# Another order of the steps from the 380th on, and state products in the upper columns of their banks

## The chip, the cores and the metric

The kernel runs on one core of a Trainium2 chip. The metric is the device time of one execution in microseconds (us), the median of several runs. The engines are named as in the profile: PE is TensorE (matmuls, with PEld for its weight loads), DVE is VectorE, ACT is ScalarE, POOL is GpSimd, and SP only issues DMAs (SPq is its queue). Each engine works through its own instructions strictly in the order in which they were written; between engines there are semaphores.

## The reference

Two blocks follow each other. The first is a gated linear attention with a state of 48 x 48 for each of 4 x 8 heads, over 768 tokens; the second is a two-layer network with a hard-swish gate, over 3072 tokens.

```python
state = alpha[:, :, t, :, None] * state + np.einsum('bhd,bhe->bhde', k[:, :, t], v[:, :, t])
y[:, :, t] = np.einsum('bhd,bhde->bhe', q[:, :, t], state)
...
h = x @ w_in                       # 3072 x 384 by 384 x 2048
g = h * np.clip(h + 3.0, 0.0, 6.0) / 6.0
return (g @ w_out).astype(np.float32)   # 2048 x 384
```

x is y with its heads side by side, 384 columns for each token. All values are float32.

## The kernel before

**Chunks and groups.** The attention goes by chunks of 128 tokens: 24 chunks j = 0 to 23, six for each of the four batches. Two chunks make a group g = j // 2 of 256 tokens for the network: 12 groups. From group 2 on (and in the second layer from group 1) the network's matrix products are done by a scheme with fewer multiplications: 20 small products in place of 24 (M, with sums of x and of weights ahead and sums of outputs behind), and 7 in place of 8 in the second layer (P).

**Steps.** The program is a text of 1788 words. Each word names a step, with its arguments behind points; `run` (L749) executes them in the order of the text under `tc.manual_schedule()`, so each engine gets its instructions in just that order, and the framework sets the semaphores that the data need. For the banks of PSUM it counts two accesses as depending on each other when they touch one bank, whatever the columns. So `M.10.9` is the tenth product of group 10, and where it stands among the PE words is when PE gets to it. The words that this text speaks of, with their lines:

- Attention, loads: `la`, `lk`, `lq` (L248; alpha, k and q of a chunk, four DMAs from chunk 6 on), `lv` (L267; v).
- Attention, on DVE: `ca`, `tk`, `tq` (L286; transposes from chunk 6 on), `r` and `p` (L309, L320; scans), `k` and `q` (L332; products with the scans), `kt` (L391; k turned back). `kw` (L393) writes the turned k to memory and `kr` (L400) reads it back by token, four DMAs each.
- Attention, products: `sc` (L338, matmuls in L346) makes the scores of a chunk in two banks, `m` (L349, L356) masks them on DVE. `u` (L422, matmuls in L429) makes the state's products of a chunk in one or two banks, `sm` (L434, L439) adds them to the state on DVE, `st` (L407, L409) decays the state on POOL, `sv` (L412, L419) places it on ACT, `qa` (L360, L366) places q on ACT. `ya` and `yb` (L448, L455) make the chunk's output y, `cy` (L461) keeps it as x on ACT.
- First layer: `xc` (L586) is one sum of x on DVE, `y` (L577) one sum of weights on DVE, `M` (L592, L600) one product, `n` (L604, L606) a copy of a product on ACT, `o` (L608; L537, L539 or L541) a sum of products on DVE, `e` (L619, L494) and `h` (L623, L498) the gate on ACT and DVE.
- Second layer: `s` (L658; L647, L664) is a sum of gated values on DVE, `P` (L685, L703) one product, `K` (L706; L682, L709) a copy on ACT, `G` (L717; L720 on ACT or L723 on DVE) an output quarter, `O` (L725) its store.
- `z` (L529, L532): dummy matmuls of the identity.

**Banks.** PSUM has eight banks of 512 float32 columns here: `banks` t0 to t3 for the attention (the last numbers of `sc`, `u`, `ya` name them) and `bank_m` m0 to m3 for the network (the last number of `M` or `P` that begins a sum). A score product takes columns 0 to 255 of its bank; y takes 0 to 383.

**What sets the order around the change.** Nothing but the text: from its 380th word (counted from zero, `y.19` in L782) it interleaves the attention of chunks 6 to 23 with the network of groups 1 to 11. The last steps are the second layer of group 11:

```python
               s.11.3.9 P.11.3.2 K.11.0.0 s.11.2.14 P.11.2 o.11.3.1 K.11.2 o.11.2.1 e.11.2.0 h.11.2
               s.11.4 e.11.3.1 h.11.3 P.11.1 G.11.0.2 s.11.5 O.11.0 K.11.1 P.11.4 G.11.1.0 P.11.5
               G.11.2.1 O.11.2 P.11.6 G.11.3.2 O.11.1 O.9.2 O.11.3""")
```

Of the kernel before, what the change touches and what calls it, by code (L numbers as in the profile page):

```python
# [17 lines left out]
def kernel(  # L18
# [33 lines left out]
    B, H, S, D = q.shape  # L52
# [4 lines left out]
    NP = H // 2  # L57
# [3 lines left out]
    G = 2  # L61
    GT = G * C
    HB = C // 2
# [42 lines left out]
    for r in range(2):  # L106
# [11 lines left out]
    st, half_st, sm = (consts.tile([C, NP, D], FP, tag=name, name=name)  # L118
                       for name in ("st", "s1", "sm"))
# [302 lines left out]
    def update(j, *at):  # L422
        for b, i in enumerate(at):
            ps_t["u", j, b] = banks[i][:, 0 : NP * D].rearrange("r (p n) -> r p n", p=NP)
        for p in range(NP):
            for a in range(2):
                for b in range(len(at)):
                    half = slice(HB * b, HB * b + HB)
                    nc.tensor.matmul(ps_t["u", j, b][64 * a : 64 * a + D, p],  # L429
                                     kb_t[j][half, p, 64 * a : 64 * a + D],  # L430
                                     v_t[j][half, b, 2 * p + a, 0:D],
                                     start=True, stop=True)
# [321 lines left out]
    with tc.manual_schedule():  # L754
# [3 lines left out]
               dx.0 w.2 d2.2 kb.1.0 ck.1 lq.1 r.2 sm.0.1 st.1 tq.1.2 q.1 d3.2 z.0.3 d1.2 dx.2  # L758
               lv.1.1 u.1.3.1 sv.1.0 sm.1.0 p.2 sm.1.1 sc.1.0.2 m.1 ya.0.3 yb.0 cy.0 lq.2 w.1 d1.1
               tq.2.1 q.2 d4.2 lk.2 tk.2.3 k.2 fa.2.0 d4.0 st.2 sc.2.0.2 d2.1 d3.1 m.2 dx.1 d4.1  # L760
               qa.1.1 lk.3 la.3 ta.3.1 ca.3 la.4 fa.0.1 sv.1.1 w.3 r.3 ta.4.3 ca.4 r.4 tk.3.1 k.3
               kb.2.0 qa.1.0 d2.3 ya.1.2 yb.1 cy.1 fa.1.2 lq.3 ck.2 d1.3 p.3 d3.3 lv.2.2 u.2.3.2
               sm.2.0 d4.3 fb.2 tq.3.1 q.3 fb.1 qa.2.0 sm.2.1 sv.2.0 st.3 fr.0.2.0 fg.0.2 lk.4
               tk.4.0 sv.2.1 w.5 d2.5 k.4 d3.5 d1.5 qa.3.0 d4.5 qa.2.1 sc.3.1.3 m.3 w.6 d2.6 d1.6
               d3.6 d4.6 lv.3.0 lq.4 w.7 kb.3.2 fb.0 f.0.3.3 kb.4.0 ya.2.1 ck.3 u.3.3.2 sm.3.0
               fr.0.3.1 fg.0.3 fr.0.1.0 fg.0.1 qa.3.1 sv.3.0 sm.3.1 p.4 d2.7 sv.3.1 d1.7 d3.7 d4.7
               f.0.5.0 fr.0.5.1 fr.0.0.0 fg.0.5 fg.0.0 tq.4.3 ck.4 la.5 ta.5.2 f.0.6.3 ca.5 w.4
               d2.4 ya.3.0 yb.3 cy.3 fr.0.6.1 yb.2 cy.2 w.9 d2.9 q.4 qa.4.1 d1.4 d1.9 dx.4 la.6 w.8
               d3.4 r.5 lk.5 w.10 d3.9 p.5 ca.6 fg.0.6 d4.9 w.12 lq.5 lv.4.1 d2.8 d3.8 f.0.7.2 d1.8
               st.4 d4.8 d4.4 w.11 fr.0.7.0 fg.0.7 f.1.7.0 fr.1.7.1 fg.1.7 sc.4.0.2 m.4 f.1.1.1  # L770
               fr.1.1.0 fg.1.1 f.1.3.3 fr.1.3.1 d2.10 d1.10 tk.5.3 f.1.0.2 d2.12 d3.10 d4.10 w.13
               fg.1.3 fr.1.0.0 fg.1.0 k.5 d3.12 lq.6 f.1.6.0 f.1.2.1 u.4.1.0 sm.4.0 d1.12 d4.12
               sv.4.0 qa.4.0 ya.4.2 fr.1.6.1 fg.1.6 w.15 tq.5.3 fa.4.3 sv.4.1 d2.11 kb.5.1 d2.13
               fr.1.2.0 f.1.4.2 fr.1.4.1 d1.11 sm.4.1 q.5 r.6 d3.11 d3.13 fg.1.4 d4.11 lv.5.0 lk.6
               tq.6 p.6 d2.15 d3.15 fg.1.2 d1.13 d4.13 sc.5.0.3 yb.4 f.1.5.0 fr.1.5.1 fg.1.5 tk.6
               m.5 b.1.0.2 fb.4 b.1.1 d1.15 d4.15 st.5 y.5 w.14 la.7 lk.7 cy.4 d2.14 qa.5.1 ck.5
               b.0.0.1 fr.0.4.0 d3.14 k.6 q.6 ca.7 fg.0.4 d1.14 d4.14 x.0 y.1 y.10 b.0.1 y.0 y.2
               u.5.2 P.1.0.0 K.1.0 qa.5.0 sv.5.0 qa.6.1 P.1.1.3 b.0.2 b.1.2 kb.6.0 ya.5.3 y.6
               s.1.0.0 sm.5.0 sv.5.1 G.1.0.0 tk.7 s.1.1.1 s.1.2.3 x.1 yb.5 cy.5 b.1.3 sc.6.1.2
               lv.6.2 ck.6 u.6.3.0 s.1.3.2 x.2 P.1.2 b.0.3 K.1.1 y.7 s.1.4 s.1.5 y.11 y.3 r.7  # L780
               xc.2.1 x.3 y.4 y.8 xc.2.3 k.7 xc.2.0 xc.2.4 y.9 y.12 y.16 y.13 y.15 P.1.3.3 K.1.2
               P.1.4 bo.1 P.1.5 xc.2.5 G.1.1.1 P.1.6 y.14 y.17 y.19 xc.2.6 sm.6.0 G.1.2.2 y.20  # L782
               M.2.0.2 lv.12.1 la.8 O.1.1 O.1.0 ca.8 y.18 y.21 y.23 so.1 G.1.3.3 n.2.0.8 bo.0 lq.7
               lv.7.0 O.1.2 m.6 xc.2.2 xc.2.10 xc.2.7 tq.7 r.8 p.7 xc.2.8 sv.6.1 M.2.15.3 M.2.1
               kb.7.3 n.2.1.9 M.2.16 M.2.2 n.2.2.10 M.2.7.0 n.2.7.11 sm.6.1 xc.2.9 q.7 p.8 M.2.3
               M.2.4 n.2.4.12 M.2.8 o.2.0.0 M.2.5 n.2.5.13 qa.7.0 sv.6.0 st.7 lk.8 O.1.3 lq.8 lk.9
               la.9 la.10 tk.8 tq.8 lq.10 lq.9 ya.6.1 yb.6 M.2.9 z.1.3 M.2.18.1 o.2.1.0 e.2.1.1
               M.2.10 cy.6 ck.7 sc.7.0.2 u.7.1.3 n.2.10.14 M.2.11 qa.7.1 ca.9 la.11 y.22 M.2.6.2
               h.2.1 q.8 m.7 e.2.0.0 h.2.0 n.2.11.15 qa.6.0 n.2.18.10 qa.8.1 M.2.12 M.2.19
               n.2.12.12 M.2.13 sm.7.0 sv.7.1 r.9 k.8 o.2.3.0 sv.7.0 ya.7.0 y.24 o.2.5.0 n.2.13.12  # L790
               o.2.2.0 yb.7 cy.7 sc.8.1.2 xc.3.1 o.2.2.1 e.2.2.1 xc.3.3 o.2.3.1 M.2.14 xc.3.4
               xc.3.0 xc.3.5 o.2.4.0 xc.3.7 xc.3.6 o.2.6.0 P.2.0.1 M.3.0.2 M.2.17 h.2.2 o.2.6.1
               e.2.3.0 h.2.3 o.2.7.0 n.3.0.12 M.3.1 n.3.1.9 e.2.5.1 M.3.7.0 n.3.7.13 xc.3.8 o.2.7.1
               K.2.0.3 xc.3.2 kt.8 e.2.6.0 h.2.6 tk.9 M.3.2 n.3.2.10 e.2.4.0 P.2.1 h.2.4 h.2.5
               s.2.0.14 e.2.7.0 G.2.0.1 h.2.7 M.3.3 M.3.4 n.3.4.8 k.9 s.2.1.11 M.3.8 o.3.0.0 ca.10
               kt.9 P.2.3.3 s.2.2.15 s.2.3.14 lv.8.2 kw.8 kr.8 lk.10 sm.7.1 xc.3.9 M.3.5 n.3.5.11
               K.2.2 e.3.0.1 xc.3.10 M.3.9 o.3.1.0 P.2.2 K.2.1 u.8.0.3 M.3.18.2 s.2.5 M.3.10
               n.3.10.14 n.3.18.15 e.3.1.0 s.2.4 P.2.4 tq.9 h.3.0 st.8 sv.8.0 M.3.11 n.3.11.8 tk.10
               p.9 sm.8.0 q.9 r.10 k.10 qa.9.0 qa.9.1 m.8 sm.8.1 h.3.1 M.3.19 o.3.5.0 kt.10 P.2.5
               G.2.2.0 st.9 M.3.12 sc.9.0.1 qa.8.0 n.3.12.10 o.3.3.0 kw.9 lv.9.0 kr.9 sv.8.1  # L800
               u.9.2.3 sm.9.0 sv.9.1 sv.9.0 G.2.1.2 sm.9.1 st.10 M.3.15.2 M.3.16 M.3.6.3 M.3.13 m.9
               o.3.4.0 o.3.6.0 tq.10 n.3.13.10 o.3.2.0 e.3.4.1 ya.8.2 yb.8 ya.9.3 yb.9 cy.9 M.3.14
               M.3.17 cy.8 xc.4.1 P.2.6 e.3.5.0 G.2.3.3 o.3.2.1 xc.4.3 h.3.4 xc.4.4 o.3.6.1 xc.4.5
               xc.4.0 xc.4.6 e.3.2.1 M.4.0.0 n.4.0.10 P.3.0.1 xc.4.7 o.3.7.0 p.10 h.3.5 o.3.3.1
               xc.4.8 M.4.7.3 M.4.1 xc.4.2 h.3.2 o.3.7.1 K.3.0.2 lk.11 O.2.2 tk.11 e.3.6.0 e.3.3.1
               h.3.3 P.3.1 e.3.7.1 n.4.1.13 M.4.2 ca.11 q.10 h.3.6 r.11 k.11 h.3.7 n.4.7.15 lv.10.2
               lv.11.0 kw.10 sc.10.0.1 kr.10 G.3.0.0 u.10.3.2 sm.10.0 qa.10.1 n.4.2.14 M.4.3 M.4.4
               M.4.8 s.3.0.9 xc.4.9 s.3.2.12 s.3.1.11 P.3.3.2 n.4.4.8 M.4.5 o.4.0.0 e.4.0.0 sv.10.1
               sm.10.1 xc.4.10 kt.11 O.2.0 O.2.3 lq.11 m.10 s.3.3.9 s.3.5 M.4.9 o.4.1.0 P.3.2
               sv.10.0 st.11 n.4.5.11 K.3.2 la.13 M.4.18.0 p.11 tq.11 lk.12 tk.12 K.3.1 M.4.10  # L810
               n.4.10.9 q.11 qa.10.0 n.4.18.12 e.4.1.1 la.12 s.3.4 ca.12 h.4.0 r.12 P.3.5 G.3.2.1
               h.4.1 M.4.11 P.3.4 n.4.11.8 M.4.12 n.4.12.14 qa.11.0 M.4.19 p.12 G.3.1.3 lq.12 kw.11
               O.2.1 tq.12 kr.11 u.11.3 sc.11.0.2 sv.11.0 O.3.1 lk.13 P.3.6 qa.11.1 M.4.6.2 G.3.3.2
               k.12 o.4.3.0 m.11 sm.11.0 sv.11.1 kt.12 M.4.13 n.4.13.14 q.12 o.4.3.1 e.4.3.0
               o.4.2.0 o.4.6.0 h.4.3 o.4.2.1 ya.10.1 ya.11.0 yb.10 yb.11 cy.11 cy.10 xc.5.1 ca.13
               xc.5.3 M.4.15.1 M.4.16 M.4.14 P.4.0.2 o.4.4.0 M.4.17 xc.5.4 o.4.5.0 xc.5.0 xc.5.5
               M.5.0.0 o.4.6.1 K.4.0.3 e.4.2.1 h.4.2 P.4.1 qa.12.1 e.4.4.0 xc.5.6 o.4.7.0 h.4.4
               o.4.7.1 tk.13 n.5.0.14 M.5.1 e.4.7.1 h.4.7 e.4.5.0 xc.5.2 h.4.5 xc.5.7 G.4.0.3
               e.4.6.1 h.4.6 s.4.1.12 s.4.0.11 xc.5.8 r.13 xc.5.9 xc.5.10 k.13 kw.12 kr.12 la.14
               sc.12.2.3 u.12.0.1 sm.12.0 n.5.1.13 M.5.2 n.5.2.15 M.5.7.1 n.5.7.8 P.4.3.3 s.4.2.9  # L820
               kt.13 lk.14 lq.13 O.3.0 O.3.3 lv.13.2 kw.13 O.4.0 lq.14 tq.13 lq.15 M.5.3 M.5.4
# [117 lines left out]
```

## Time and profile before

| What | us |
|---|---|
| runs of the kernel | 537.21, 537.83, 538.51 (median 537.83) |
| the profiled execution | 537.71 |
| its span, from the first to the last instruction | 535.6 |
| PE busy in the span | 523.6 |
| DVE busy in the span | 475.1 |
| ACT busy in the span | 259.7 |
| first PE step behind the 380th word (M.2.0) starts | 125.42 |
| end of the last matmul | 532.69 |

An instruction's row gives its start and its length in us, then engine, line, operation, the tiles written and read, and how many were merged in the row; in brackets stands how long the engine was idle ahead of it and what ended that. PE's matmuls overlap: a row of sixteen L703 matmuls is 2.76 us long, but the next row starts 2.60 us behind its start. So times of PE are taken here from start to start.

### The profile page before, as it was taken

The page shows a single profiled execution, that of the slowest core. Times are in us where ns is not written, and L with a number is a line of the kernel's source. Part 1 is how long each engine was busy: PE and PEld are TensorE (multiplying, and loading weights), DVE is VectorE, ACT ScalarE, POOL GpSimd, SP SyncE. Part 2 cuts the span into 40 slices and gives each one's busy share as a digit, 9 for nine tenths or more (in the row PEclk, how much of TensorE's full clock was granted, in tenths as well). Part 3 has the DMA queues.
Part 4 walks back from the last instruction along what each step waited for, and adds up shares of the span by engine and source line. Part 5 has one row for each costly group of instructions (what it writes and reads, how often), then busy time and mean ns, then how long its engine had stood idle before and what let it go on. Part 6 is the DMA issues. An engine that isn't in the chain of part 4 may idle for free.

```text
span 535.6 us, 15166 instructions
## 1 busy us (share of the span) xinstructions
PE 523.6 (98%) x6306; PEld 497.0 (93%) x6306; DVE 475.1 (89%) x839; ACT 259.7 (48%) x513; POOL 50.4 (9%) x71
## 2 busy tenths in 40 slices
PE   7799999999999999999999999999999999999997
PEld 7698886789999999999999999999999999999996
DVE  6999989999999899989999899999999898595381
ACT  3889864302753644543644444642634545553240
POOL 5333435000000000000010000000000000000000
PEclk9999999999999999999999999999999999999999
DMA  9998877006515155254354355055354042100001
GB/s 175 214 250 263 205 218 164 9 1 162 151 28 121 29 120 134 51 139 90 92 118 104 89 122 141 20 126 124 85 137 103 17 97 48 43 3 1 15 16 37
DMA packets 124100, 54.40 MB, mean 102 GB/s; under 512 B 83328, under 2 KB 116864, under 8 KB 124032
## 3 DMA queue, kind: packets, MB, share of 16 engines
q1 hardware_dynamic: 124032, 53.44, 42.4%
q8 instruction: 49, 0.80, 0.7%
q14 instruction: 19, 0.16, 0.1%
HBM read 44.50 MB, written 8.91 MB: 100 GB/s over the span
## 4 chain that ended last, share of the span: by engine, by line
PE 64%; DVE 20%; SPq 5%; DMA 3%; issue 3%; ACT 2%; POOL 2%; DVEq 0%; ACTq 0%; POOLq 0%
PE m_ps L703 28%; PE m_ps L600 24%; PE m_ps L478 4%; SPq L262 3%; PE t_ps L455 3%; DVE R L309 2%; DVE g_sb L498 2%; DVE A L356 2%; DMA v<-in_v_dram 1%; PE t_ps L346 1%; PE m_ps L516 1%; PE t_ps L429 1%; DVE g_sb L537 1%; DVE q L332 1%; DVE t L286 1%
## 5 line engine op out<-in xcount | busy, mean ns | idle before, releaser
L703 PE MATMUL m_ps<-w,g_sb 128*128 128x192 f32 x704 | 122.1, 327 | 0.7 <-ACT m_ps L709 0.6
L606 ACT COPY g_sb<-m_ps 128x512 f32<-128x512 f32 x110 | 63.5, 584 | 113.8 <-PE m_ps L600 97.4
L703 PEld LDWEIGHTS m_ps<-w,g_sb 128*128 128x128 f32 x704 | 113.7, 190 | 1.8 <-ACT m_ps L709 0.9
L703 PE MATMUL m_ps<-rings,g_sb 128*128 128x192 f32 x528 | 91.6, 327 | 0.6 <-ACT u L682 0.6
L703 PEld LDWEIGHTS m_ps<-rings,g_sb 128*128 128x128 f32 x528 | 85.3, 190 | 1.0 <-ACT u L682 0.9
L600 PE MATMUL m_ps<-xc,w 128*128 128x128 f32 x640 | 82.8, 277 | 0.5 <-DVE w L541 0.5
L600 PEld LDWEIGHTS m_ps<-xc,w 128*128 128x128 f32 x640 | 77.5, 192 | 1.7 <-issue 0.6
L494 ACT ACTIVATE r<-g_sb,half 128x512 f32<-128x512 f32 x80 | 56.7, 722 | 29.5 <-DVE g_sb L541 11.7
L498 DVE SCALAR_TENSOR_TENSOR g_sb<-r,g_sb 128x512 f32<-128x512 f32 x80 | 53.6, 683 | 7.2 <-ACT r L494 6.8
L600 PE MATMUL m_ps<-xT,raw 128*128 128x128 f32 x400 | 52.6, 278 | 1.0 <-ACT g_sb L606 0.9
L600 PEld LDWEIGHTS m_ps<-xT,raw 128*128 128x128 f32 x400 | 48.6, 192 | 2.0 <-ACT g_sb L606 1.4
L409 POOL TENSOR_TENSOR st<-sm,R 128x192 f32<-128x192 f32 x20 | 12.9, 644 | 354.4 <-DVE sm L439 305.6
L647 DVE TENSOR_TENSOR g_sb<-g_sb 128x512 f32<-128x512 f32 (+1 forms) x55 | 42.0, 792 | 1.4 <-PE m_ps L703 1.1
L600 PE MATMUL m_ps<-xT,w 128*128 128x128 f32 x320 | 42.0, 276 | 0.0
L600 PEld LDWEIGHTS m_ps<-xT,w 128*128 128x128 f32 x320 | 39.3, 192 | 0.1
L366 ACT COPY A<-q 48x256 f32<-48x256 f32 x88 | 35.6, 404 | 4.9 <-DVE q L332 3.7
L356 DVE TENSOR_TENSOR A<-t_ps,mask 64x256 f32<-64x256 f32 x96 | 36.0, 413 | 0.4
L478 PE MATMUL m_ps<-xT,w 128*128 128x256 f32 x144 | 32.8, 382 | 0.1
L600 PE MATMUL m_ps<-xc,raw 128*128 128x128 f32 x240 | 31.8, 276 | 0.0
L309 DVE TENSOR_TENSOR_SCAN R<-t,ones 128x516 f32<-128x516 f32 x24 | 29.6, 1235 | 1.1 <-ACT t L300 1.0
L478 PEld LDWEIGHTS m_ps<-xT,w 128*128 128x128 f32 x144 | 26.7, 190 | 3.8 <-POOL w L217 0.2
L600 PEld LDWEIGHTS m_ps<-xc,raw 128*128 128x128 f32 x240 | 29.6, 192 | 0.1
(105 smaller groups left out, 724.8 us busy)
## 6 DMA issues: line engine op xcount, KB each, us to landing
raw<-in_moe_w_out_dram SPq DMA_DIRECT2D x8, 768.0 KB, 5.2
raw<-in_moe_w_in_dram SPq DMA_DIRECT2D x6, 768.0 KB, 6.7
v<-in_v_dram SPq DMA_DIRECT2D x48, 96.0 KB, 3.0
out_dram<-oh SPq DMA_DIRECT2D x44, 96.0 KB, 1.7
far<-kq SPq DMA_DIRECT2D x64, 64.0 KB, 2.2
kb<-far SPq DMA_DIRECT2D x64, 64.0 KB, 2.0
aq<-in_alpha_dram SPq DMA_DIRECT2D x36, 96.0 KB, 2.4
qq<-in_q_dram SPq DMA_DIRECT2D x36, 96.0 KB, 2.4
```

The source lines that it names most:

```text
L262: nc.sync.dma_start(out=to[BLK * o : BLK * (o + 1), :, 0 : V * D - skip], in_=t[o // 2, :, :, skip : V * D])
L309: nc.vector.tensor_tensor_scan(out=reverse(R, n - 1, n), data0=reverse(ax, n, n), data1=reverse(ones, n, n), initial=0.0, op0=ALU.mult, op ...
L356: nc.vector.tensor_tensor(out=to[:, a], in0=sc[a][half], in1=mask[half, half].unsqueeze(1).to_broadcast([HB, NP, HB]), op=ALU.mult)
L366: nc.scalar.copy(out=to[:, a], in_=Q_t[j][64 * a : 64 * a + D, :, half])
L455: nc.tensor.matmul(y_of(j, (i + 1) // 2, p)[:, HB * b : HB * b + HB], vb[:, p, e : e + 32], A_t[j][:, b, 2 * p + a], start=(b == 0 and i = ...
L478: nc.tensor.matmul(h[:, f], w1[:, kk, o : o + C], xT_t[g][:, kk], start=(kk == 0), stop=(kk == KT - 1))
L494: nc.scalar.activation(out=to, in_=h, func=AF.Relu, bias=half, scale=1.0 / 6.0)
L498: nc.vector.scalar_tensor_tensor(out=to, in0=r, scalar=1.0, in1=h, op0=ALU.min, op1=ALU.mult)
L600: nc.tensor.matmul(acc[g][i][:, f * C : (f + 1) * C], spots[w][:, f * C : (f + 1) * C], x_of(g, x), start=(first and f == 0), stop=last, s ...
L606: nc.scalar.copy(out=slots[z], in_=acc[g][i])
L647: nc.vector.tensor_tensor(out=out, in0=in0, in1=in1, op=ALU.subtract)
L703: nc.tensor.matmul(to[g], a, rhs[:, f], start=(first and f == 0), stop=(last and f == HF - 1), skip_group_check=True)
```

## The change

Two things change. `update` writes the state's products into columns 256 to 447 of their banks; they were in columns 0 to 191.

```diff
     def update(j, *at):
         for b, i in enumerate(at):
-            ps_t["u", j, b] = banks[i][:, 0 : NP * D].rearrange("r (p n) -> r p n", p=NP)
+            ps_t["u", j, b] = banks[i][:, NP * HB : NP * (HB + D)].rearrange(
+                "r (p n) -> r p n", p=NP)
         for p in range(NP):
```

(NP is 4, HB 64, D 48.) This adds a line, so that lines behind L424 have a number higher by one afterwards.

And the words from the 380th on stand in another order. Both texts have the same 1788 steps; the first 380 are the same words (on other line breaks). Behind them no step is added or removed, and 46 steps have another bank at their end: 16 of `ya`, 16 of `sc`, 14 of `u`. The start of the new part, and places that the text speaks of:

```diff
-               P.1.4 bo.1 P.1.5 xc.2.5 G.1.1.1 P.1.6 y.14 y.17 y.19 xc.2.6 sm.6.0 G.1.2.2 y.20
-               M.2.0.2 lv.12.1 la.8 O.1.1 O.1.0 ca.8 y.18 y.21 y.23 so.1 G.1.3.3 n.2.0.8 bo.0 lq.7
-               lv.7.0 O.1.2 m.6 xc.2.2 xc.2.10 xc.2.7 tq.7 r.8 p.7 xc.2.8 sv.6.1 M.2.15.3 M.2.1
...
+               la.8 xc.2.2 xc.2.6 y.19 G.1.3.3 so.1 y.20 G.1.2.2 y.18 M.2.0.2 bo.0 y.21 M.2.15.3
+               y.23 sm.6.0 n.2.0.8 z.1.3 M.2.1 M.2.16 xc.2.8 n.2.1.9 xc.2.7 M.2.2 kb.7.3 p.7 lk.8
...
```

In words, for the rest: the dummy `z.1.3` stood between M.2.9 and M.2.18 and stands ahead of M.2.1. Score and state products of a chunk, which had banks of their own, share banks in many chunks (`u.7.1.3 sc.7.1.3`, `u.12.3.0 sc.12.3.0`, `u.14.3.0 sc.14.3.2`, `u.20.1.2 sc.20.1.0`). Chunk 21's part is `u.21.3.2 sc.21.1.0 n.9.11.11 M.9.15.3 sm.21.0 M.9.12 G.8.1.0 lk.23 ya.20.3 yb.20 m.21 sm.21.1` and, seven words on, `ya.21.1 yb.21`. The end is

```python
P.11.3.2 O.10.3 s.11.4 P.11.2 P.11.1 s.11.5 K.11.1 P.11.4 G.11.0.2 K.11.2 G.11.1.0
O.11.1 P.11.5 O.11.0 G.11.2.1 P.11.6 O.11.2 G.11.3.2 O.11.3
```

Most steps have moved by some tens of words or fewer, some loads, stores and placements on ACT by over a hundred.

## The prediction

> **What bounds the kernel now.** I read the busy shares first, then the busy times by stretch, the waits of TensorE (PE), the waits of VectorE (DVE), and the timeline where a wait stood out.
>
> ```profile
> PE 523.6 (98%) x6306; PEld 497.0 (93%) x6306; DVE 475.1 (89%) x839; ACT 259.7 (48%) x513; POOL 50.4 (9%) x71
> ...
> 240.00:280.00 40.00, 40.00 (x471) 39.60 (x472) 38.78 (x71) 17.40 (x35) 1.82 (x3) 1.00 0.42 96
> 320.00:360.00 40.00, 40.00 (x513) 39.41 (x511) 38.01 (x70) 19.30 (x42) 0.80 (x1) 1.00 0.40 96
> 400.00:440.00 40.00, 40.00 (x520) 39.11 (x519) 37.29 (x69) 17.95 (x38) 1.03 (x2) 1.00 0.32 71
> 480.00:500.00 20.00, 20.00 (x150) 20.00 (x149) 10.96 (x18) 7.12 (x14) 0.00 (x0) 1.00 0.00 1
> ```
>
> In the stretches the columns after the length are PE, PE weight loads, DVE, ACT, POOL. PE hardly rests from 120 us on, and its granted clock is 1.00 throughout. But DVE is at least 93% busy until 440 us, and only behind 460 us has it room: two engines bound this part, and PE sets the end only while DVE keeps up.
>
> ```profile
> PE m_ps L600 <- ACT g_sb L606: 0.9, 1, 0.9
> PE m_ps L703 <- ACT u L682: 0.6, 1, 0.6
> PE m_ps L703 <- ACT m_ps L709: 0.6, 2, 0.4
> PE m_ps L600 <- DVE w L541: 0.5, 1, 0.5
> ```
>
> These are all the named waits of PE matmuls from 94 us on: 2.6 us. I price them by start-to-start times: a group of eight L600 matmuls takes 0.89 us, sixteen of L703 take 2.60. What exceeds that is lost: 0.63 us at 126.3 (M.2.15 to M.2.1), 0.27 at 155.2 (M.3.2 to P.2.1), 0.32 at 195.9 (in P.3.1), 1.06 at 277.7 (P.5.1 to M.6.2), 0.41 at 443.1 (to P.9.1) and 0.79 at 521.2 (P.11.1 to P.11.4), 3.48 in all. Passing to the small matmuls (L346, L429, L455) and back costs about 0.1 us each way (a group of eight takes 0.99 ahead of them and 1.00 behind them).
>
> **The first term, a filler moved into a hole.**
>
> ```profile
> 126.31 1.06 PE L600 MATMUL m_ps<-xT,raw 128*128 128x128 f32 x8
> 127.84 1.13 PE L600 MATMUL m_ps<-xc,w 128*128 128x128 f32 x8 [0.47 <-DVE w L541]
> ...
> 137.71 0.83 PE L532 MATMUL m_ps<-ident 128*128 128x128 f32 x6
> ```
>
> M.2.1 waits until 127.84 for a weight sum on DVE. The dummy z.1.3 (six L532, 137.71 to 138.38, 0.67 us) now stands just ahead of M.2.1. PE is free at 127.20, the dummy ends at 127.87, and 0.60 us is saved where it stood. On DVE the sums ahead of it change by one short xc added and one sm put behind (0.24 for 0.31), so it is not later.
>
> **The second, the tail.**
>
> ```profile
> 521.23 2.76 PE L703 MATMUL m_ps<-w,g_sb 128*128 128x192 f32 x16
> 524.03 0.32 ACT L720 COPY oh<-m_ps 128x192 f32<-128x192 f32 x1 [3.65 <-PE m_ps L703]
> 524.24 0.33 ACT L682 COPY u<-m_ps 128x192 f32<-128x192 f32 x1
> 524.62 2.87 PE L703 MATMUL m_ps<-rings,g_sb 128*128 128x192 f32 x16 [0.63 <-ACT u L682]
> ```
>
> P.11.4 overwrites what K.11.1 copies (L682), and ACT reaches that copy only behind the output copy G.11.0 (L720), which waits for P.11.1. In the new order K.11.1 stands ahead of G.11.0: its input is ready 2.60 us earlier, at the end of P.11.2, so the copy lies beside P.11.1. DVE, counted from the last M.11.14 with 0.63 to 0.68 per step, has s.11.4 some 3 us ahead of P.11.4. Saved: 0.79.
>
> **The third, fewer passages.** PE's new order has 26 stretches of small matmuls behind step 380 for 28: 2 x 0.2 = 0.4 us.
>
> **The fourth, the other holes.** 0.27 + 0.32 + 1.06 + 0.41 = 2.06 us. Each is a short chain from PE over ACT or DVE back to PE. The new order has as many chains that the PE work between leaves less than 0.9 us to spare (22 for 22, counted with the mean durations of the readers' groups). Between 0 and 2.06 of this goes.
>
> If all went, PE alone would give 0.60 + 0.79 + 0.4 + 2.06 = 3.85 us less. The profiled execution took 537.71 us, 0.12 under the median of the runs (537.83), with a span of 535.6. So the floor is 533.9.
>
> **What works against it: DVE's queue.** The same DVE work stands in another order, and PE must not pass a step before DVE has done all that is queued ahead of its input. I added DVE's work behind step 380 in both orders with durations from back-to-back rows (two h steps 1.29 us, a scan 1.15, a transpose 1.03, four mask products 1.51), and PE's with those above. The before trace then tells at what time DVE had done so much, and when PE had.
>
> At P.8.2, 279.0 us of PE work stands ahead in both orders; ahead of its input s.8.3 stand 289.2 us of DVE work before and 291.1 after. At ya.21 it is 296.8 of PE against 306.4 of DVE before, 293.3 against 305.4 after: PE comes there at the time 427.0 of the old trace, DVE ends its mask at 430.1, 3.1 us late. The worst is M.10.9, which waits for o.10.0.0: 319.4 us of PE work (454.1) against 331.0 of DVE work (457.6), 3.5 us late, where the old order had 3.6 us to spare. Other late places are 1.8 us at P.9.1 and 1.2 at M.8.0, covered by the worst. (P.8.2 reads s.8.3 only in its second half, 1.3 us in, and is just not late.)
>
> This takes DVE to idle as before. It idled 15.7 us between 120 and 440 (320 less the busy times of the stretches). Its largest named waits, from 94 to 430 us:
>
> ```profile
> DVE g_sb L498 <- ACT r L494: 4.2, 5, 1.5
> DVE g_sb L537 <- PE m_ps L600: 2.0, 3, 1.0
> DVE oh L723 <- PE m_ps L703: 1.5, 1, 1.5
> DVE oh L723 <- ACT A L366: 1.4, 1, 1.4
> DVE xc L537 <- ACT xT L464: 1.0, 1, 1.0
> ```
>
> They are waits for inputs that PE and ACT make; a DVE that runs 1 to 3 us later meets them less. From 320 us on, where the new order has it late, the ones above 0.35 us are 1.09, 1.04, 0.43, 0.40, 1.49 and 0.54, 5.0 in all. The cut in idle lies between 0 (the waits come back at other steps) and 6.6 (PE's floor: 3.5 + 0.6 + 0.4 + 2.06). I take four fifths of 5.0: 4.0. That pays the 3.5 and leaves 0.5 of the terms ahead of 454 us; the 0.79 comes behind it. The sum: 537.71 + 3.5 - 4.0 - 0.79 = **536.4 us**.
>
> **The bank move.** update() now writes columns 256 to 447 of its bank, score products 0 to 255. It changes no instruction's size: cost of itself 0. It lets PE write both into one bank with no wait on a reader between. The built program's waits show the price: in chunks 7, 12, 14 and 20 the first sum of state (L439) waits for the score matmuls in the shared bank, up to 0.51 us (L346, 302.06 to 302.58) each, 2.0 us of DVE's idle at most, 0 where DVE has other work until then. No row of before shows a shared bank.
>
> [...]
>
> **Queues of SP and POOL.** The 16 chunks' k go through memory (kt on DVE, kw, kr on SP, then u). Before, the last read was issued 5.7 us or more behind kt and landed 2.0 later: 7.7 us at least. By the ledger the time from kt to u falls from 12.3 us at least to 8.8 (chunk 23), 9.6 (13), 9.8 (19), 9.9 (18): all hidden, with 1.1 us at the closest. Loads of alpha, k and q keep 14 us or more between the freeing of their buffer and use. The stores that moved on SP (the longest wait of SP is 39.8 us, behind the last load) stand behind outputs that are long done or in the tail. POOL (9% busy) hides st: 0.
>
> **Rivals.**
> - DVE stays as idle as before and PE waits at ya.21 and M.10.9. The early terms vanish in that wait: 537.71 + 3.5 - 0.79 = 540.4. For it: the late DVE is sure by the count. Against: waits on inputs shrink when the reader comes later. It turns slower than before once less than 2.7 us of idle is cut. 18%.
> - Half paid: idle falls by 1.5 to 3.7 us, which gives 538.9 to 536.7: no change that can be measured. 24%.
> - Shared banks: the four waits of 0.51 fall in idle DVE time, the cut is 4.0 - 2.0 = 2.0, time 538.4; with the half-paid case's lower cut, 539 or more. 6%, half of it slower.
> - k late: a store's wait of 3 us ahead of a read makes the four close chunks 1.9, 1.1, 0.9 and 0.8 us late, 4.7 in all, so 537.71 + 4.7 - 1.9 of gains = 540.5. Against: spare of 1.1 us, stores ready. 7%.
> - The new order does what it is laid out to do on both engines: 533.9 to 535.5. It needs over 4.9 us of idle cut. 18%.
>
> **How the numbers follow.** A difference under 0.2% (1.1 us) can't be told from none here (runs of before spread 0.24%). The forecast (535.5 to 536.8, 27%) and the best case (18%) are faster: 45%, with 2% of near misses of half-paid, 47%. Same: 22 + 3 = 25%. Slower: 18 + 3 + 7 = 28%. The range reaches from the floor, 533.9, to the first rival, 540.4. The forecast's side has its own range, 533.9 to 536.8.
>
> **What will show it.** Right: no hole ahead of M.2.1 and P.11.4, the L532 matmuls at 127 us, DVE busy 38.5 or more of each 40 us from 320 to 440. Wrong: PE waits on L439, L356 or L537 of DVE between 400 and 460 us; idle of PE ahead of L429 with a DMA as releaser; a wait of L439 for L346.

## The result, and the profile after

The changed kernel takes 534.80 us (median of 6 runs beside 6 of the kernel before, 537.75): a ratio of 0.9952, 95% interval 0.9941 to 0.9962. The forecast was 536.4, its range 533.9 to 540.4. The profiled execution took 535.22 us, its span is 533.4 against 535.6. In the rows of after, L601 is the L600 of before, L704 is L703, and L533 is L532.

The busy shares of the kernel after, and its busy times by stretch (start and end, length, then TensorE, its weight loads, VectorE, ScalarE, GpSimd, the granted clock, the DMA share):

```profile
PE 522.5 (98%) x6306; PEld 496.9 (93%) x6306; DVE 475.9 (89%) x839; ACT 261.3 (49%) x513; POOL 49.5 (9%) x71
...
240.00:280.00 40.00, 39.04 (x520) 38.27 (x519) 37.67 (x70) 20.04 (x43) 1.84 (x3) 1.00 0.45 109
320.00:360.00 40.00, 40.00 (x542) 39.27 (x541) 38.44 (x71) 18.77 (x39) 1.58 (x2) 1.00 0.41 98
360.00:400.00 40.00, 40.00 (x554) 39.43 (x552) 36.92 (x67) 18.91 (x40) 0.54 (x2) 1.00 0.41 97
400.00:440.00 40.00, 39.87 (x491) 38.88 (x492) 38.50 (x70) 19.49 (x43) 1.31 (x2) 1.00 0.36 82
```

VectorE does more in the same time: over 120 to 440 us its busy times add to 308.7 of 320, so it idles 11.3 us where it idled 15.7. TensorE has lost 0.96 us in the stretch from 240, which was full before.

The waits of TensorE's matmuls from 94 us on (what waits, for whom; us in total, times, longest), all of them:

```profile
PE m_ps L601 <- issue: 1.4, 2, 1.0
```

Every named wait of before is gone. What is left are two waits for nothing that the profile names. The timeline shows where they stand:

```profile
224.92 1.99 PE L456 MATMUL t_ps<-A,v 128*32 128x64 f32 x128
226.84 0.94 PE L601 MATMUL m_ps<-xT,raw 128*128 128x128 f32 x6
228.26 1.38 PE L601 MATMUL m_ps<-xT,raw 128*128 128x128 f32 x10 [0.48 <-issue]
...
262.72 2.00 PE L456 MATMUL t_ps<-A,v 128*32 128x64 f32 x128
264.64 1.27 PE L601 MATMUL m_ps<-xc,w 128*128 128x128 f32 x9
266.87 0.94 PE L601 MATMUL m_ps<-xc,w 128*128 128x128 f32 x7 [0.96 <-issue]
```

Both lie inside a run of equal matmuls on equal operands, behind 128 of the smallest ones (L456). The sixth matmul of the first run starts at 227.50 and takes its turn of 0.11 us; the seventh starts at 228.26, 0.65 us late. By start to start of the steps, the measure of the prediction, the two cost 0.85 and 1.12 us; 0.1 of the 0.85 is the passage behind small matmuls (1.00 for 0.89 us for a group of eight in the kernel before).

The first two terms of the prediction, in the same timeline:

```profile
126.63 1.06 PE L601 MATMUL m_ps<-xT,raw 128*128 128x128 f32 x8
127.52 0.83 PE L533 MATMUL m_ps<-ident 128*128 128x128 f32 x6
128.19 1.06 PE L601 MATMUL m_ps<-xc,w 128*128 128x128 f32 x8
...
519.98 2.76 PE L704 MATMUL m_ps<-w,g_sb 128*128 128x192 f32 x16
...
520.18 0.32 ACT L683 COPY u<-m_ps 128x192 f32<-128x192 f32 x1 [4.26 <-PE m_ps L704]
...
522.58 2.76 PE L704 MATMUL m_ps<-rings,g_sb 128*128 128x192 f32 x16
```

The groups follow each other at 0.89, 0.67 and 2.60 us: no hole ahead of M.2.1, none ahead of P.11.4.

From the start of M.2.0 to the end of the last matmul it is 404.81 us against 407.27, 2.46 less; this measure (called the late part below) leaves out the first 125 us, which no edit past step 380 touches and which differ by 0.6 us between the profiles of kernels with the same steps there (M.2.0 starts at 125.42 to 126.07). By start to start, the 2.46 are: holes of over 0.15 us, 3.58 before (the prediction's 3.48 and 0.10 at 155 us, there put down to a passage) and 3.20 after, 0.38; two stretches of small matmuls fewer, 0.4; and 1.69 in gaps of about 0.1 us and less.

Much of the 1.69 lies inside the stretches of small matmuls. From the first small matmul to the start of the first large one behind, a stretch of 32 L346 and 32 L429 matmuls took 0.98 to 1.50 us before (13 of them); after, each of the 11 takes 0.98 or 0.99. What the old ones took above 0.98, with 0.3 in a mixed stretch at 146 us, adds to 1.4 us. The hole at P.9.1 (0.41) is in this and already in the 3.58, so some 1.0 us is left of it: short waits, most of them under the 0.15 us from which the views name a wait. The remaining 0.7 I cannot assign to a cause.

Of the 3.20, 1.97 are the two holes with no name, 0.39 stands at P.8.2 (411 us) and 0.84 at 148 to 156 us.

### The profile page after: what moved, and what is told of

It reads as the page before. It is cut to its first block, busy times and chain, and to the rows that moved or that the text cites. A ratio compares the mean times of both kernels' runs of the same rounds, so it can differ in the third digit from the quotient of the medians.

```text
span 533.4 us, 15111 instructions
## 1 busy us (share of the span) xinstructions
PE 522.5 (98%) x6306; PEld 496.9 (93%) x6306; DVE 475.9 (89%) x839; ACT 261.3 (49%) x513; POOL 49.5 (9%) x71
## 4 chain that ended last, share of the span: by engine, by line
PE 80%; DVE 14%; issue 2%; DMA 1%; POOL 1%; ACT 1%; SPq 0%; DVEq 0%; ACTq 0%; POOLq 0%
PE m_ps L704 33%; PE m_ps L601 29%; PE m_ps L479 6%; PE t_ps L456 4%; PE m_ps L490 2%; PE t_ps L346 2%; PE t_ps L430 2%; DMA v<-in_v_dram 1%; DVE g_sb L648 1%; PE m_ps L517 1%; PE t_ps L282 1%; DVE rings L648 1%; DVE R L309 1%; DVE A L356 1%; DVE g_sb L538 1%
## 5 line engine op out<-in xcount | busy, mean ns | idle before, releaser
L704 PE MATMUL m_ps<-w,g_sb 128*128 128x192 f32 x704 | 121.5, 326 | 0.0
L704 PEld LDWEIGHTS m_ps<-w,g_sb 128*128 128x128 f32 x704 | 113.8, 190 | 0.3
L704 PE MATMUL m_ps<-rings,g_sb 128*128 128x192 f32 x528 | 91.7, 327 | 0.1
L704 PEld LDWEIGHTS m_ps<-rings,g_sb 128*128 128x128 f32 x528 | 85.3, 190 | 0.5 <-DVE g_sb L648 0.4
L601 PE MATMUL m_ps<-xc,w 128*128 128x128 f32 x640 | 83.9, 277 | 1.0 <-issue 1.0
L601 PEld LDWEIGHTS m_ps<-xc,w 128*128 128x128 f32 x640 | 78.0, 192 | 2.1 <-issue 1.0
L495 ACT ACTIVATE r<-g_sb,half 128x512 f32<-128x512 f32 x80 | 57.0, 722 | 28.4 <-DVE g_sb L499 11.2
L601 PE MATMUL m_ps<-xT,raw 128*128 128x128 f32 x400 | 53.1, 277 | 0.5 <-issue 0.5
L601 PEld LDWEIGHTS m_ps<-xT,raw 128*128 128x128 f32 x400 | 48.9, 192 | 1.2 <-issue 0.7
L601 PE MATMUL m_ps<-xT,w 128*128 128x128 f32 x320 | 42.0, 277 | 0.0
L601 PEld LDWEIGHTS m_ps<-xT,w 128*128 128x128 f32 x320 | 39.1, 192 | 0.4
L601 PE MATMUL m_ps<-xc,raw 128*128 128x128 f32 x240 | 32.1, 277 | 0.1
L538 DVE TENSOR_TENSOR g_sb<-g_sb 128x512 f32<-128x512 f32 x40 | 27.1, 680 | 4.9 <-ACT g_sb L607 4.9
L601 PEld LDWEIGHTS m_ps<-xc,raw 128*128 128x128 f32 x240 | 29.8, 192 | 0.6 <-DVE xc L540 0.4
```

Of the source, the lines that this page charges most:

```text
L495: nc.scalar.activation(out=to, in_=h, func=AF.Relu, bias=half, scale=1.0 / 6.0)
L538: eng.tensor_tensor(out=out, in0=in0, in1=in1, op=ALU.add if s1 > 0 else ALU.subtract)
L601: nc.tensor.matmul(acc[g][i][:, f * C : (f + 1) * C], spots[w][:, f * C : (f + 1) * C], x_of(g, x), start=(first and f == 0), stop=last, s ...
L704: nc.tensor.matmul(to[g], a, rhs[:, f], start=(first and f == 0), stop=(last and f == HF - 1), skip_group_check=True)
```

## The experiments

"Late part" is the measure above, from each run's own profile. The kernel before took 537.75 us beside the first of them and 537.41 to 537.46 beside the others.

| run | median us | ratio, 95% interval | late part us |
|---|---|---|---|
| changed kernel | 534.80 | 0.9952 (0.9941 to 0.9962) | 404.81 |
| the same again | 534.81 | 0.9948 (0.9936 to 0.9960) | 404.11 |
| 25 small matmuls (100 records) | 533.49 | 0.9931 (0.9919 to 0.9944) | 403.22 |
| 64 small matmuls (256 records) | 538.46 | 1.0025 (1.0008 to 1.0041) | 405.12 |
| more VectorE work at 411 us | 536.95 | 0.9990 (0.9981 to 0.9999) | 406.64 |
| more VectorE work at 475 us | 536.36 | 0.9976 (0.9967 to 0.9986) | 406.43 |
| before, two moves | 536.59 | 0.9983 (0.9974 to 0.9992) | 406.28 |
| dummy put back | 535.87 | 0.9967 (0.9954 to 0.9979) | 404.93 |
| before, bank move alone | 537.42 | 1.0002 (0.9993 to 1.0010) | 407.21 |
| before, less VectorE work | 537.65 | 1.0004 (0.9995 to 1.0013) | 407.32 |
| 25 small matmuls, h.9.0 later | 534.51 | 0.9940 (0.9927 to 0.9952) | 403.11 |
| 25 small matmuls, q load earlier | 533.75 | 0.9926 (0.9914 to 0.9939) | 403.14 |
| q load earlier | 534.72 | 0.9943 (0.9930 to 0.9957) | 404.84 |

### The holes with no name: instruction blocks that land late

TensorE's records in the trace, counted from the first, give a lead: the holes end at records 5569 and 6593, which are 4 x 256 apart. The profile's DMA queue table has a queue for instructions with 49 packets and 0.80 MB, 16 KB each, and TensorE has some 12,700 records, 49.7 x 256. So I read a packet as a block of 256 records. The trace's packet for the first of the two blocks went from 225.59 to 226.87, that for the second from 264.53 to 265.50; the matmuls went on 1.39 and 1.37 us after the landing. From the start of the block ahead to the end of the hole it is 3.3 and 4.0 us. Without the holes (0.64 and 1.12 us between two matmuls) those blocks would, by subtraction, be run through in 2.6 and 2.9 us; the 128 matmuls of L456 are 256 records in 1.9 us.

The test shifts all later block boundaries by 100 records:

```diff
+    tiny = lambda n: [nc.tensor.matmul(bank_m[0][0:D, 0:D], ident[0:D, 0:D], ident[0:D, 0:D],
+                                       start=True, stop=True) for _ in range(n)]
-               u.1.3.1 sv.1.0
+               t.25 u.1.3.1 sv.1.0
```

> The changed kernel with 25 matmuls of 48x48 (100 records of TensorE's instruction stream) put ahead of u.1.3.1, where TensorE stood idle 0.95 us at 19.7 us; nothing reads what they write. Theory A, the two holes with no wait (0.85 us up to 228.26, 1.12 us up to 266.87) are instruction blocks that landed late, and TensorE alone sets the end: all later block boundaries come 100 records earlier in the stream, away from the stretches of small matmuls at 225 and 263 us; both holes vanish and the time falls by 1.97 us, 534.8 to 532.8. Theory B, late blocks too, but VectorE is the second limit: both holes vanish, the wait at P.8.2 (0.39 us at 411 us) grows towards 2.4 us, and the time falls by 0 to 0.6 us. Theory C, the holes are waits that the records leave out: they stay at the same matmuls, and the time is that of the changed kernel within 0.3 us.

In the profile of this run no wait of TensorE's matmuls is left at all, and the place at 227 us reads:

```profile
224.82 1.99 PE L456 MATMUL t_ps<-A,v 128*32 128x64 f32 x128
226.74 2.05 PE L601 MATMUL m_ps<-xT,raw 128*128 128x128 f32 x16
```

The 16 matmuls run through, and the second hole is gone too. The late part falls by 1.59 us and the median by 1.3, most of theory A's 1.97: matmul for matmul the two holes give 0.73 and 1.12, and 0.24 is lost again at 242 us. Theory B fails: P.8.2's wait stays at 0.38 us though TensorE comes there 1.6 us earlier. VectorE followed: from 240 to 280 us it is busy 38.92 us in place of 37.67. So it had been waiting for TensorE there.

Did the boundaries do it, or the small matmuls? If it was the boundaries, a shift by 256 records leaves the holes where they were:

```diff
-               u.1.3.1 sv.1.0 sm.1.0 p.2 sm.1.1 sc.1.0.2 m.1 ya.0.3
+               t.32 u.1.3.1 sv.1.0 sm.1.0 p.2 sm.1.1 sc.1.0.2 m.1 t.32 ya.0.3
```

> The changed kernel with 64 small matmuls in place of 25 (32 ahead of u.1.3.1, 32 ahead of ya.0.3): 256 records, a whole instruction block, so every later block boundary falls on the same matmul as in the changed kernel. Late instruction blocks: the holes at 227 and 266 us are back (0.8 to 1.1 us each), and from M.2.0 on the time is the changed kernel's; in all 534.8 and up to 1.0 for what the matmuls themselves take ahead of 25 us. If the small matmuls helped in another way than by moving the boundaries (an earlier clock, warmer tables), the holes are gone as with 25 of them, and the time is about 533.5.

The holes are back at the same matmuls, 0.91 and 0.83 us, and the late part is 405.12:

```profile
235.80 1.38 PE L601 MATMUL m_ps<-xT,raw 128*128 128x128 f32 x10 [0.54 <-issue]
274.12 0.94 PE L601 MATMUL m_ps<-xc,w 128*128 128x128 f32 x7 [0.67 <-issue]
```

The boundaries did it. The time itself missed its expectation, 538.5 for at most 535.8. Blocks came late in the first 45 us too: the profile has start gaps of 2.70 and 1.07 us at 34 and 42 us, at record counts 961 and 1217, both again 193 more than a multiple of 256, and 1.3 us behind the landing of a packet. This profile is the slowest of the ten runs (543.01); it comes to M.2.0 7.5 us later than the changed kernel's, of which these two gaps are 3.2. The dummies themselves and what else they delay are not told apart.

> The changed kernel unchanged, so that the three runs beside it have it on the same chip. All theories: 534.8 us within 0.5; the hole ahead of M.4.16 at 227 us stands (it stood in every profile whose order up to there was this one), the one ahead of M.5.17 at 266 us in most.

Here the first hole stood (0.94) and the second did not. Over all six profiles with these boundaries (the changed kernel twice, more VectorE work twice, dummy put back, q load earlier) the first stood six times, 0.85 to 1.07 us, the second four times. Where the second was missing, its packet had started over 0.5 us ahead of the start of the block before it, as in the run with work at 475 us (262.27, block from 262.89), in place of 1.1 to 1.7 us behind it. So a part of the spread of the changed kernel's runs (534.07 to 536.37, where the kernel before has 537.21 to 538.51) may be whether a block comes in time; each kernel has one profile, so the runs do not show it. The kernel before has such a block at the same place, 2.3 us long from 225.88, and no hole behind it: the packet for the next one had started at 224.28, 1.6 us ahead of it.

### Is VectorE the second bound?

Two operations that write ones over ones, once where the ledger says that VectorE is just in time, once where it has room:

```diff
+    spend = lambda n: [nc.vector.tensor_tensor(out=ones, in0=ones, in1=ones, op=ALU.max) for _ in range(n)]
-               M.9.9 s.8.3.14
+               M.9.9 v.2 s.8.3.14
```

> The changed kernel with two more VectorE operations of 128x516 (about 0.68 us each, 1.36 together; they write ones over ones) ahead of s.8.3.14, the sum that P.8.2 waits 0.39 us for. Theory B, VectorE's work sets the end here: P.8.2's wait grows to about 1.7 us and the time by 1.0 to 1.4 us, 534.8 to 536.0. Theory A, TensorE alone sets the end and VectorE has room: under 0.3 us is left of it at the end. The order up to P.8.2 is that of the changed kernel, so the holes at 228.26 and 266.87 should stand again in this profile, if they come from the order and not from chance.

The same with `v.2 xc.11.1` in place of `xc.11.1`:

> The changed kernel with the same two VectorE operations (1.36 us together) put late, ahead of xc.11.1, where VectorE is busy 28.4 of 40 us. All theories: 534.8 within 0.4 us, nothing of it is left at the end; if the time grows by 1 us or more, the added operations cost something other than VectorE's room, and the run that put them ahead of s.8.3.14 says nothing of VectorE.

In the first, P.8.2 now stands still in its middle:

```profile
411.76 1.47 PE L704 MATMUL m_ps<-rings,g_sb 128*128 128x192 f32 x8
414.63 1.57 PE L704 MATMUL m_ps<-rings,g_sb 128*128 128x192 f32 x8 [1.41 <-DVE g_sb L648]
```

By start to start, P.8.2's loss grew from 0.39 to 1.68 us, 1.29 for 1.36 of work. At this place VectorE's queue does set TensorE's pace. But the late part grew by 1.83, more than was added, and the second kernel's by 1.62 where 0 was expected. That control failed, and by its own condition the times of the pair then say nothing of VectorE; only the timelines do. They show two things that have nothing to do with the added work's place, and one that has. In the first kernel:

```profile
381.24 1.11 DVE L286 STREAM_TRANSPOSE q<-qq 128x512 f32<-128x512 f32 x1 [1.21 <-DMA qq<-in_q_dram]
```

VectorE waits for the load of q; in the second it waits 1.3 us at the same step. By P.8.2, TensorE is 0.5 and 0.7 us behind the changed kernel in the two. The second kernel has, besides:

```profile
275.44 0.28 PE L430 MATMUL t_ps<-v,kb 64*48 64x48 f32 x2
276.57 0.53 PE L430 MATMUL t_ps<-v,kb 64*48 64x48 f32 x28 [0.85 <-DMA kb<-far]
...
477.38 2.87 PE L704 MATMUL m_ps<-w,g_sb 128*128 128x192 f32 x16 [0.35 <-DVE g_sb L542]
```

Here the late block at 266 was missing, TensorE came to u.14 1.1 us earlier, and met k's way through memory 0.9 us late: what the one hole gave, the other took (the rival "k late", at a chunk that the prediction had not listed). And at 477 P.10.0 waits for a sum behind the added work: 0.61 us of the 1.36 reach TensorE, although VectorE is busy only 28.4 of 40 us there. A busy share of 71% did not mean that this sum had room. So the pair shows 1.3 us at P.8.2 and 0.6 at P.10.0, and not the contrast that was wanted.

The kernel before with less VectorE work:

```diff
-        "p": growth,
+        "p": lambda j: P_t.__setitem__(j, Ps) if j in (13, 14) else growth(j),
```

> The kernel before without the growth scans of chunks 13 and 14 (2.44 us of VectorE at 249 and 273 us; both chunks use chunk 12's products instead, so the output is not the reference's). Theory B, VectorE's deliveries set TensorE's pace in the order before: the hole ahead of M.6.2 (1.06 us at 277.7) closes and so do later ones, and 1.0 to 1.5 us are kept, 537.5 to 536.2. Theory A, the holes come from the order of the steps and not from VectorE's load: the hole stays, and so does the time, within 0.3 us.

Theory A: nothing is gained, and the hole ahead of M.6.2 stands as before:

```profile
278.38 2.77 PE L703 MATMUL m_ps<-w,g_sb 128*128 128x192 f32 x16
282.05 1.16 PE L600 MATMUL m_ps<-xT,raw 128*128 128x128 f32 x8 [0.90 <-ACT g_sb L606]
```

In the order before, this hole does not come from VectorE's load: it ends with a copy of ScalarE, and 2.44 us of VectorE's time bought nothing (late part 407.32 for 407.27). Only the scans at 249 and 273 us were taken out, so VectorE's load ahead of them is not tested.

### The two moves alone

```diff
 (the order before)
-   M.2.15.3 M.2.1          M.2.9 z.1.3 M.2.18.1       G.11.0.2 s.11.5 O.11.0 K.11.1 P.11.4
+   M.2.15.3 z.0.3 M.2.1    M.2.9 M.2.18.1             K.11.1 G.11.0.2 s.11.5 O.11.0 P.11.4
```

> The kernel before with two of the moves alone: three idle matmuls taken from the stretch ahead of M.2.18 and put ahead of M.2.1, and K.11.1 put ahead of G.11.0.2. Theory A, TensorE sets the end, so both steps of the prediction are kept in full: -0.60 and -0.79, 537.7 to 536.3. Theory B, VectorE sets the end between 140 and 480 us: the 0.60 is given back at the next wait for VectorE, and 0.79 is left, 536.9.

536.59 lies midway between the two theories; the late part, 0.99 us shorter, and the timeline speak for theory B. The tail's move keeps 0.90 us. Of the dummy's 0.60, 0.02 is left at 139 us and 0.09 at the end of the late part:

```profile
127.66 0.83 PE L532 MATMUL m_ps<-ident 128*128 128x128 f32 x6
128.33 0.41 PE L600 MATMUL m_ps<-xc,w 128*128 128x128 f32 x2
...
139.61 1.16 PE L600 MATMUL m_ps<-xc,w 128*128 128x128 f32 x8 [0.40 <-DVE g_sb L541]
```

The hole ahead of M.2.1 is filled, and M.2.18, ahead of which the dummy stood, now waits for its own VectorE step. The dummy had been filling a hole there too.

The opposite, in the changed kernel:

```diff
-   n.2.0.8 z.1.3 M.2.1   ...   k.8 M.2.18.1
+   n.2.0.8 M.2.1   ...   k.8 z.1.3 M.2.18.1
```

> The changed kernel with the three idle matmuls put back from the place ahead of M.2.1 to that ahead of M.2.18, where the order before had them. Theory A, TensorE's lost time is kept to the end: a hole of about 0.6 us stands again ahead of M.2.1 and the time is 535.4. Theory B, TensorE waits for VectorE at the next places anyway: the hole is there, the waits up to 156 us (0.22, 0.29 and 0.33 us) shrink by as much, and the time stays within 0.2 us of 534.8.

Neither theory: there is no hole ahead of M.2.1 without the dummy.

```profile
126.44 1.06 PE L601 MATMUL m_ps<-xT,raw 128*128 128x128 f32 x8
127.34 1.10 PE L601 MATMUL m_ps<-xc,w 128*128 128x128 f32 x8
```

The next two lines are VectorE's, from the same profile and from that of the kernel before, and show why:

```profile
126.13 0.69 DVE L542 SCALAR_TENSOR_TENSOR w<-w 128x512 f32<-128x512 f32 x1
```

```profile
127.00 0.69 DVE L541 SCALAR_TENSOR_TENSOR w<-w 128x512 f32<-128x512 f32 x1
```

The sum that M.2.1 waited for begins 0.6 us behind M.2.0's start (125.55) where it began 1.6 behind (125.42). The new order had moved VectorE's sum, and that alone closed the hole. Nor is there a hole ahead of M.2.18 for the dummy to fill: TensorE stands 0.04 us behind the changed kernel there and level with it at 156 us. So in the new order the dummy's 0.67 us are spent at either place; no run leaves it out. The late part is 404.93, 0.12 more than the changed kernel's, which can't be told from none; the median, 535.87, is 1.07 more, with overlapping intervals, and its profile shows no place for so much.

### The bank move alone

The line of the diff at L424, in the kernel before with its own order.

> The kernel before, its own order, with the state update's products in columns 256 to 448 of their banks in place of 0 to 192: the bank move alone. Both theories: no change, 537.7 within 0.3 us, since no product of this order shares a bank with scores. If matmuls or reads at other columns cost something else, it shows here: 96 of each 2 x 24 products and sums would have to differ by 10 ns each to show 0.5 us.

As expected: 1.0002, with 0.1% either way. In this order no product shares a bank; what the sharing is worth in the new order, no run took alone.

### Two repairs

P.8.2's wait is left, so h.9.0 was put behind the sum that P.8.2 reads (in this run h.9.0 reads its buffer after s.8.3 has overwritten it, so a part of group 9 is computed from other numbers):

```diff
-   M.9.5 st.21 h.9.0 M.9.9 s.8.3.14 o.9.1.0
+   M.9.5 st.21 M.9.9 s.8.3.14 h.9.0 o.9.1.0
```

> The changed kernel with the 25 small matmuls ahead of u.1.3.1 (533.5 us) and, besides, h.9.0 (0.69 us of VectorE) put behind s.8.3.14 instead of ahead of it. If VectorE's queue alone makes P.8.2 wait (0.38 us), the sum comes 0.6 us earlier, the wait vanishes and the time falls to 533.1 us. If that sum waits for TensorE's own products, the wait stays, and the time with it.

The wait is gone and 0.11 us is left of it in the late part: TensorE gained 0.36 and lost 0.26 again within 4 us, at P.8.5. The median, expected at 533.1, is 534.51 against 533.49, with overlapping intervals. That buffer is why h.9.0 has to stand first.

The load of q that VectorE waited for needs only a buffer that has been free since 338 us, yet it stood in SyncE's queue behind the reads of kr.19 and the loads of k and alpha, four DMAs each, which go out one behind the other from 368.9 to 374.9 us in the changed kernel; its own four go out from 375.5 us:

```diff
-   kr.19 lk.21 p.19 ca.20 P.7.2 la.22   ...   M.8.5 lq.20 sv.18.1 lq.21
+   kr.19 lq.20 lk.21 p.19 ca.20 P.7.2 la.22   ...   M.8.5 sv.18.1 lq.21
```

> The changed kernel with only the load of q for chunk 20 put ahead of that of k for chunk 21. VectorE's wait at 380 us (0 in the changed kernel's first profile, 1.0 to 1.3 us in those of three variants) is gone. If it makes the changed kernel's runs spread from 534.1 to 536.4 us, they now lie within a microsecond and the median falls by 0.2 to 0.6 us; if the spread comes from instruction blocks that land early or late, it stays.

> The changed kernel with the 25 small matmuls, and the load of q for chunk 20 put ahead of that of k for chunk 21 in SyncE's queue. VectorE waited for this load at 380 us, 0.4 us with the 25 matmuls and 1.0 to 1.3 us in three other runs of this order. If that wait reaches TensorE (0.2 us at M.8.18 and 0.1 to 0.4 us around P.8.2 where it was over a microsecond), the time is 533.2 to 533.5 us; if not, 533.5. The wait for the load is gone in both.

In both the wait for q is gone. Alone it is worth nothing that can be measured (534.72). Its runs, from 533.99 to 535.30, spread more than those of the changed kernel beside it (534.73 to 535.08), so the spread is not the load's. With the 25 matmuls it gives 533.75, and its five runs, 533.37 to 533.96, all lie below the fastest of the 11 of the changed kernel (534.07). This version is faster than both kernels. So is the one with the 25 matmuls alone (533.49), by its late part, 1.59 us shorter; its interval (0.9919 to 0.9944) just touches the changed kernel's. Between the two nothing can be told.

## Why the prediction was right, and where it was not

- **The forecast.** Faster, as forecast, and 1.6 us more of it. The reason given (TensorE's holes go while VectorE keeps up) holds in part. The prediction's holes went, but others came, so that holes of over 0.15 us make only 0.38 of the 2.46 us; some 1.0 us came from the short waits inside stretches of small matmuls, for which the prediction had no term. It had none for the two late blocks either, which cost 1.85 us the other way. That the sum came as near as it did is in part luck.
- **The floor, 533.9, or 3.85 us less.** It was none: with 25 small matmuls ahead, the same order has a late part 4.05 us shorter than before (403.22 for 407.27), and 1.2 us of waits are left in it (0.84 and 0.38). The holes that the floor was built on left out the short waits.
- **The term that was mis-sized: the cut in VectorE's idle,** "four fifths of 5.0: 4.0". By the ledger o.10.0.0 would end at 457.6 with idle as before. It ended at 452.51, and M.2.0 had started 0.32 later than before: 5.4 us were cut. Of these the lateness of 3.5 is paid, and 1.9 are left: TensorE stands 1.5 ahead of the old trace at M.10.9 (452.90 for 454.1, and the 0.32), and the sum is there 0.4 before it is needed. The forecast had left 0.5. This 1.0 us is most of the miss of 1.6; 0.2 came behind M.10.9, and 0.4 is the median of the runs against the profiled execution (534.80 and 535.22).
- **Why it was mis-sized.** I counted VectorE's idle as a store to draw on. Part of it is TensorE's lateness seen from the other side: with the two late blocks gone, VectorE idled 1.25 us less from 240 to 280 us, and TensorE kept 1.6. So the ledger's late places say where TensorE can be held up (P.8.2, "just not late", lost 0.39 and passed on 1.29 of 1.36 us; M.10.9 had 0.4 to spare), but not how much.
- **First term, 0.60 by the dummy.** The hole closed; the cause was wrong. VectorE's sum came 1.0 us earlier in the new order, which I had read as "not later". The dummy's move alone is worth less than 0.1 in the order before, and nothing that can be told in the new one.
- **Second term, the tail, 0.79.** Right: 0.90 alone, and no hole.
- **Third, two stretches of small matmuls fewer.** They are gone; their 0.4 comes from the count, no run took it alone.
- **Fourth, the other holes, between 0 and 2.06.** All four went, and others came: 0.22, 0.29 and 0.33 at 148 to 156 us (waits for xc.3.5, o.2.6.1 and n.3.1) and 0.39 at P.8.2, 1.23 in all, and the two late blocks, 1.97 by the same measure, which no step of the prediction had.
- **Bank move, 0.** Right for the columns alone: 1.0002. The four waits for scores in shared banks, and so the rival, do not show: no wait of L440 (L439 before) of 0.2 us or more is among VectorE's from 94 to 430 us.
- **SyncE's queue.** "All hidden" held for the changed kernel's profile. It was nearer than the count: k was 0.9 us late at chunk 14 once TensorE came early, and q up to 1.3 us late at chunk 20. The count took buffer to use and left out the queue: the buffer of that q was free at 338 us, and its load went out from 375.5, behind twelve DMAs that went out from 368.9 to 374.9.
- **The signs.** No hole ahead of M.2.1 and P.11.4, L533 at 127 us: seen. VectorE busy 38.5 of each 40 from 320 to 440: 38.44, 36.92, 38.50, so only in part. None of the signs against it was seen in the changed kernel's profile.

VectorE's waits from 94 to 430 us in the kernel after, beside those shown of before:

```profile
DVE g_sb L499 <- ACT r L495: 2.4, 3, 1.4
DVE xc L540 <- PE m_ps L601: 1.3, 2, 0.9
DVE g_sb L538 <- ACT g_sb L607: 1.2, 3, 0.5
DVE g_sb L540 <- PE m_ps L601: 0.7, 2, 0.5
```

The waits for ScalarE's r fell from 4.2 to 2.4 us, and the two for outputs (oh, 1.5 and 1.4) are gone. The second line is the wait behind the late block at 266 us.

## What to carry to other kernels

Where two engines feed each other and are both over 90% busy, as here from 120 to 440 us, do not sum up idle time (4.0 us were reckoned from VectorE's, 5.4 were cut): ask of each hole which queue it waits for, and try the move alone, since a filler that is moved can uncover what it had filled, as here, where 0.02 of the dummy's 0.60 us was left at 139 us. A hole inside a run of equal matmuls, with no releaser, is worth a count of the engine's records: here the holes ended 4 x 256 records apart, and a shift by 100 records closed both, where one by 256 left both. And take a load's spare time from its place in the queue, not from the freeing of its own buffer: the q of chunk 20 had its buffer from 338 us on and still kept VectorE waiting 1.2 and 1.3 us at 380 us in the two runs with more VectorE work.

## What the runs showed of the hardware

The changed kernel's profile has 49 instruction packets of 16 KB. Taken in order, the n-th landed ahead of TensorE's record 193 + 256n, for all 48 such records in the trace. The two that landed closest ahead of theirs, 1.39 us (record 5569) and 1.37 us (record 6593), are those of the two holes; the next closest, 1.89 us (record 10689, at 426.61 us), left none. In the kernel before, which has no such hole from 94 us on, the closest of 49 is 2.08 us.

In all twelve holes of seven profiles (the six with the changed kernel's boundaries and the one with 64 small matmuls) the packet started 0.6 to 0.8 us after TensorE had begun the block ahead of it, or 1.1 to 1.7 us at the second place; it took 1.0 to 1.4 us to land, and the block's first matmul began 1.3 to 1.6 us behind that. These blocks started 3.3 to 4.0 us behind the one ahead of them, which holds 128 matmuls of L456 (1.9 us for 256 records), and a hole of 0.8 to 1.1 us was left. In the kernel with 25 small matmuls a block of 3.4 us at 346 us left none: its successor landed 1.73 us ahead of its first matmul. What decides whether a packet starts that late is open; at the second place it changed between runs of one kernel.
